# A gated mix of a recurrent-memory transformer and a GEGLU layer: one buffer for Q and K rows, P kept where P^T is written, the gate carried in the rows of b, and part of one more weight piece kept on the chip

## The chip, the cores and the metric

The kernel runs on one core of one Trainium2 chip. The metric is the device time of one launch in microseconds (us). Times of the kernel before are the median of six runs; the profile is one further execution.

## What is computed

The input x has 2048 rows of 640 numbers. Branch a cuts it into 64 segments of 32 rows. Each segment is put behind 8 memory rows, goes through attention with 32 heads of 192, and hands the first 8 rows of its result to the next segment as memory, so the segments are a strict chain. Branch b is a GEGLU layer over all rows. The output is g*a + (1-g)*b with one gate number for each row.

```python
g = sigmoid((x * gate_w).sum(-1, keepdims=True))
for s in range(64):                                # branch a
    h = concat([mem, x[:, 32*s:32*s+32]], axis=1)  # 8 + 32 = 40 rows
    q, k, v = h @ Wq, h @ Wk, h @ Wv               # 640 -> 32 heads x 192
    p = softmax(where(mask, q @ k.T * 192**-0.5, -1e9))
    o = einsum('bhte,hed->btd', p @ v, Wo)
    mem = o[:, :8];  outs.append(o[:, 8:])
b = (gelu(x @ w_gate) * (x @ w_up)) @ w_down       # branch b
return g * a + (1 - g) * b
```

## The kernel before, in words

**Order of the work.** A small scheduler (`_Sched`) takes every operation with the regions that it reads and writes, puts it on its engine's stream in program order and adds the semaphore waits. Nothing is reordered: what stands first on an engine's stream holds back what stands behind it. DMAs are issued from two streams, SP's (weights) and ACT's (`AUXQ`: scratch, b, output).

**Prologue.** Branch b comes first, in four blocks of 512 rows (`ffn_gu` and `ffn_down`, L791 to L830). `ffn_down` multiplies with `w_down` in a part of 512 columns, read out by ACT (L820), and one of 128, read out by DVE (L824); (1-g)*b goes to a scratch tensor in HBM (L828). The gate column `gcol` is spread afterwards by `gate_spread` (L731): eight small DMAs on SP build a table `gseg` with one column for each segment. Then comes the "left" phase (L880 to L908): Q and K of the last 8 rows of each segment's x, which no memory touches, for all segments at once, stored in HBM by L906. Resident weights are loaded by L656 in three classes: 35 pieces during branch b, 14 after it, 13 at the start of the first segment.

**Weights.** The four matrices are cut into 84 pieces: Wq, Wk and Wv into 4 "octs" of 5 pieces each (384 KB), Wo into 24 pieces (320 KB). They do not all fit. 62 are resident, two are "held" in PSUM and copied into SBUF buffers that are idle at that moment (L619 at q 0 and k 0, L632 at `pw`), and 20 are streamed anew for every segment through a ring of five slots (`issue_ring`, L576). A slot is loaded again when the matmuls on its old piece are done, so a piece is issued when the piece five places ahead of it has been used. A loop over estimated times (`COST`, `tcons`) picks the 20. It takes these, as (matrix, oct, piece) or (3, Wo piece): (0,0,3), (1,0,4), (0,1,1), (1,1,0), (1,1,4), (0,2,3), (1,2,1), (2,2,0), (0,3,1), (1,3,0), (2,3,0), (2,3,4), and Wo 2, 5, 8, 11, 15, 18, 21, 23.

**A segment.** The list `PROG` gives the order: q, k, v of an oct (L947, L967), with the scores (`sc`, L1009), exponent (`ex`, L1036), transposed P (`pt`, L1061), P times V (`pv`, L1087) of earlier octs between them, and Wo (L1110) at the end.

- Q and K rows: ACT copies PSUM into `rows_sb` (L951), Q into one buffer, K into another; DVE transposes each (`tq`, `tk`, L957) for the scores.
- Softmax: DVE takes the maximum and subtracts (L1024, L1026), ACT takes the exponent, DVE sums, inverts and multiplies into `p_sb` (L1043; for oct 3 L1045 and L1046). `p_transp` transposes on PE and DVE masks the result into `PTm` and `PTl` (L1064, L1067), from which `pv_oct` multiplies; ACT and DVE read its result out (L1091, L1097, L1098).
- End of a segment: DVE casts the 8 memory rows (L1155), PE transposes them (L1165), DVE writes them into H (L1170), and the next segment's q can start. Then L1176 mixes g*a into the rows of b; `out_store` sends them out, issued behind K of oct 0 of the next segment. V of oct 1 uses the same bytes as these rows, so its read-out (L978) waits for that store to land.
- GpSimd fills the left rows of Q and K from the staging buffer `stg` (L927, L929).

Every fourth segment computes V of the left rows as well (L991).

Of the kernel before, what the change touches and what calls it, by code (L numbers as in the profile page):

```python
# [221 lines left out]
def _build(nc, A_x, A_mem0, A_Wq, A_Wk, A_Wv, A_Wo, seg_len, w_gate, w_up, w_down,  # L222
# [17 lines left out]
    R = L + M  # L240
# [22 lines left out]
    b_scr = nc.dram_tensor("ffn_b_scratch", (S, Dm), BF, kind="Internal").ap()  # L263
# [4 lines left out]
    total = int(nc.sbuf_bytes_remaining) - 64  # L268
    total -= total % 64
# [8 lines left out]
    wsA["small"] = al(NSEG * 4 + 8 + 32 + 16)  # L278
    HD = Dm // 2
    wsA["ident"] = al(128 * 2)  # L280
    wsA["maskm"] = al(R * 2)
# [3 lines left out]
    wsB["rows"] = al(2 * 768)  # L285
    wsB["stg"] = al(NOCT * 2 * LW * 2)
# [5 lines left out]
    wsB["p"] = al(4 * 64 * 2)  # L292
    wsB["stats"] = al(2 * 3 * 4 * 4)
# [12 lines left out]
    ffn_sz["brow"] = al(NBR * Dm * 2)  # L306
# [4 lines left out]
    res_cap = total - wsA_total - wsB_total - ring_bytes  # L311
# [11 lines left out]
    assert o == ring_bytes + res_cap  # L323
# [24 lines left out]
    for k, n in (("gseg", 0), ("mbd", 4 * NSEG), ("mle", 4 * NSEG + 8), ("gwT", 4 * NSEG + 40)):  # L348
        wsA_off[k] = wsA_off["small"] + n
# [7 lines left out]
    gseg = fview(wsA_off["gseg"], 4 * NSEG)  # L357
    r_gseg = sreg(wsA_off["gseg"], 4 * NSEG)
# [4 lines left out]
    gwT = bview(wsA_off["gwT"], KT * 2)  # L363
    r_gwT = sreg(wsA_off["gwT"], KT * 2)
# [12 lines left out]
    rowb = bview(o_rowb, HD * 2)  # L377
    r_rowb = sreg(o_rowb, HD * 2)
# [11 lines left out]
    rows_sb = [bview(wsB_off["rows"] + b * 768, 768) for b in range(2)]  # L390
    r_rows = [sreg(wsB_off["rows"] + b * 768, 768) for b in range(2)]
    stg = bview(wsB_off["stg"], NOCT * 2 * LW * 2).rearrange("p (o m b i) -> p o m b i", m=2, b=6, i=2 * M)
    stg_flat = bview(wsB_off["stg"], NOCT * 2 * LW * 2)
    r_stg = sreg(wsB_off["stg"], NOCT * 2 * LW * 2)
# [4 lines left out]
    p_sb = bview(wsB_off["p"], 512).rearrange("p (t k) -> p t k", k=2 * L)  # L399
    pm_sb = bview(wsB_off["p"], 256).rearrange("p (t k) -> p t k", k=L)  # L400
    pl_sb = bview(wsB_off["p"] + 256, 256).rearrange("p (t k) -> p t k", k=L)
    r_p = sreg(wsB_off["p"], 512)
# [8 lines left out]
    st_f = [[fview(wsB_off["stats"] + (3 * b + i) * 16, 16) for i in range(3)] for b in range(2)]  # L411
    r_st = [sreg(wsB_off["stats"] + 48 * b, 48) for b in range(2)]
    assert NVB * 768 >= Dm * 2
    mem0r = bview(wsB_off["v"], Dm * 2)
    r_mem0r = sreg(wsB_off["v"], Dm * 2)
# [26 lines left out]
    brow = [bview(ffn_off["brow"] + b * Dm * 2, Dm * 2) for b in range(NBR)]  # L442
    r_brow = [sreg(ffn_off["brow"] + b * Dm * 2, Dm * 2) for b in range(NBR)]
# [31 lines left out]

    def piece_size(key):
        return GO if key[0] == 3 else GQ

    def piece_view(key, o):
        if key[0] == 3:  # L480
# [5 lines left out]
            ("q", 2), ("pt", 0), ("sc", 1), ("tq", 2), ("ex", 1), ("k", 2), ("tk", 2), ("pv", 0), ("v", 2),  # L486
            ("q", 3), ("pt", 1), ("sc", 2), ("tq", 3), ("ex", 2), ("k", 3), ("tk", 3), ("pv", 1), ("v", 3),
# [33 lines left out]
    HELD2 = (0, 1, 4)  # L521

# [4 lines left out]
    nstream = 0  # L527
    while True:
        streamed = set()
        for k in range(nstream):  # L530
            target = (k + 0.5) * tseg / nstream
            best = min((i for i in range(npieces) if i not in streamed and i not in held_i and may_stream(order[i])), key=lambda i: abs(tcons[i] - target))
            streamed.add(best)
        if tot_bytes - GO - GQ - sum(piece_size(order[i]) for i in streamed) <= res_cap:
            break
        nstream += 1
# [26 lines left out]
    r_ring = [sreg(o, GQ) for o in ring_off]  # L563
    order_index = {key: i for i, key in enumerate(order)}
# [6 lines left out]
    def issue_ring(seg, upto):  # L571
        done = issued.get(seg, 0)
        while done <= upto:
            key = order[stream_list[done]]
            slot = stream_counter[0] % B_RING
            S_.add("sp", lambda e, slot=slot, key=key: e.dma_start(piece_view(key, ring_off[slot]), piece_src(key)),  # L576
                   writes=[r_ring[slot]], dma_sem="ring%d" % slot, name="ring s%d p%d" % (seg, done))
            stream_counter[0] += 1
            ring_of[(seg, key)] = slot
            done += 1  # L580
        issued[seg] = done

    def piece(seg, key):
# [13 lines left out]
        slot = ring_of[(seg, key)]  # L597
        return piece_view(key, ring_off[slot]), r_ring[slot]
# [10 lines left out]
    o_held = wsB_off["rows"] + al(2 * 768) - GO  # L609
    assert o_held >= wsB_off["Q"] and o_held + 1024 >= wsB_off["rows"]  # L610
# [3 lines left out]
    assert o_held2 + GQ <= wsB_off["p"] + 256  # L614
# [44 lines left out]
    def load_residents(cls):  # L659
        for key in order:  # L660
# [70 lines left out]
    def gate_spread():  # L731
        S_.add("pool", lambda e: e.memset(gseg, 0.0), writes=[r_gseg], name="gate zero")
        for i in range(8):
            q, h = i % 4, i // 4
            S_.add("sp", lambda e, q=q, h=h: e.dma_start(gseg[64 * h + M:64 * h + R, NG * q:NG * q + NG], gcol[L * q:L * q + L, :]),
                   reads=[r_gcol], writes=[sreg(wsA_off["gseg"] + 8 * i, 8)], dma_sem="gl", name="gl%d" % i)

# [67 lines left out]
    def ffn_down(blk):  # L805
        n1 = min(Dm, 512)
        for a in range(FA):
# [3 lines left out]
            for f in range(FT):  # L811
                fns.append(lambda e, f=f, a=a, xb=xb: e.matmul(ps[:, xb, 0:n1], hT_sb[:, f, a * 128:(a + 1) * 128], wd_sb[:, f, 0:n1],  # L812
                                                               start=(f == 0), stop=(f == FT - 1)))
                if Dm > 512:
                    fns.append(lambda e, f=f, a=a, yb=yb: e.matmul(ps[:, yb, 0:Dm - 512], hT_sb[:, f, a * 128:(a + 1) * 128], wd_sb[:, f, 512:Dm],
                                                                   start=(f == 0), stop=(f == FT - 1)))
            wr = [r_ps[xb]] + ([r_ps[yb]] if Dm > 512 else [])
# [5 lines left out]
            if Dm > 512:  # L823
                S_.add("dve", lambda e, bs=bs, yb=yb, a=a: e.tensor_scalar(  # L824
                    out=brow[bs][:, 512:Dm], in0=ps[:, yb, 0:Dm - 512], scalar1=gtmp[:, 4 + a:5 + a], scalar2=None,
                    op0=ALU.mult), reads=[r_ps[yb], r_gtmp], writes=[r_brow[bs]], name="ffn b evac2")
            row0 = blk * FB + a * 128
            S_.add(AUXQ, lambda e, bs=bs, row0=row0: e.dma_start(b_scr[row0:row0 + 128, :], brow[bs]),  # L828
# [19 lines left out]
    gate_spread()  # L848
    held_buf = {HELD2: (wsB_off["Q"], wsB_off["vl"]), HELD: (wsB_off["uT"], wsB_off["stg"])}
    for a_, b_ in zip(("Q", "vl", "uT", "stg"), ("stg", "uT", "stats", "vl")):  # L850
        assert wsB_off[b_] - wsB_off[a_] >= GQ
# [70 lines left out]
    def stg_load(s):  # L922
        S_.add(AUXQ, lambda e: e.dma_start(stg_flat, qkl[s]), reads=[Rg("qk", 64 * o_ + s, 64 * o_ + s + 1) for o_ in range(NOCT)],
               writes=[r_stg], dma_sem="stg", name="stg s%d" % s)

    def left_fill(s, o):
        S_.add("pool", lambda e: e.tensor_copy(out=Qs[:, :, L:R].rearrange("p b r h -> p b (r h)"), in_=stg[:, o, 0]), reads=[r_stg], writes=[r_Ql],  # L927
               name="Ql s%d o%d" % (s, o))
        S_.add("pool", lambda e: e.tensor_copy(out=Ks[:, :, L:R].rearrange("p b r h -> p b (r h)"), in_=stg[:, o, 1]), reads=[r_stg], writes=[r_Kl],  # L929
# [99 lines left out]
    def softmax(s, o):  # L1029
# [18 lines left out]
        S_.add("dve", fns, reads=[rb, rst], writes=[r_p], name="smax p")  # L1048

    def p_transp(s, o):  # L1050
        bank = 5 + o % 2
# [20 lines left out]
    def pv_oct(s, o):  # L1072
# [17 lines left out]
        S_.add("pe", fns[8:], reads=[r_v[o % NVB], r_vl[o], r_PTm, r_PTl], writes=[r_ps[B]], name="PVb s%d o%d" % (s, o))  # L1090
        S_.add("act", lambda e: e.activation(  # L1091
# [182 lines left out]
```

## Time and profile before

| | us |
|---|---|
| six runs, median (lowest to highest) | 1890.12 (1885.56 to 1901.77) |
| the profiled execution, its own time | 1898.12 |
| its span, first to last instruction | 1896.4 |
| branch b, until the left phase starts | 0 to 175.7 |
| left phase, until the first segment's matmuls | 175.7 to 300.3 |
| first segment, until its memory rows | 300.3 to 342.4 |
| 62 segments, from memory rows to memory rows | 342.4 to 1869.4, 24.63 each |

The mean granted TensorE clock is 0.986. PE is busy for 93% of the span, DVE 49%, ACT 47%, GpSimd 8%. Busy PE is no measure of distance from the end: its ends are modelled, and it says nothing of which wait comes last. The rows to read are the waits of PE, by what ended them, and the timeline of one segment. The segments differ: the shortest takes 22.5 us, the longest 27.07; those that compute the left rows' V take 25.72 in the mean.

### The profile page before, as it was taken

Reading aid. Unit: us, or ns where it says so; the run is one execution under the profiler, and the core shown is the slowest. Engines: PE = TensorE matmul, PEld = TensorE weight load, DVE = VectorE, ACT = ScalarE, POOL = GpSimd, SP = SyncE. Lnnn points to the kernel's source line nnn. Section 1 sums busy time; section 2 is a strip of 40 time slices with the busy share of each in tenths; the row PEclk is TensorE's granted clock in tenths of the full one; section 3 lists DMA queues with packets and bytes.
Section 4 is the critical chain, followed back from the end, with each engine's and each line's share of the span. In section 5 each row is a group of like instructions: output and inputs, shape, how many; then the busy total and the mean of one; then the engine's idle time right before and its main releaser. Section 6 shows DMA issues by size and latency. Waiting matters only on the chain.

```text
span 1896.4 us, 79908 instructions
## 1 busy us (share of the span) xinstructions
PE 1755.1 (93%) x34856; PEld 1173.8 (62%) x34864; DVE 937.1 (49%) x2944; ACT 882.0 (47%) x2093; POOL 145.1 (8%) x547
## 2 busy tenths in 40 slices
PE   8999796999999999999999999999999999999998
PEld 4456684666666666666666665666666666666665
DVE  3222243555555555555555545555555555555555
ACT  2222233555444454554454444555555555554454
POOL 1000000000000000000000000000000000000000
PEclk9999898999999999999999999999999999999999
DMA  9512658999999999989999989999999999999998
GB/s 364 215 32 73 195 159 247 310 325 320 317 315 321 309 309 316 317 298 324 307 325 305 310 289 313 295 311 325 322 316 325 321 314 327 324 319 301 309 318 281
DMA packets 281737, 551.03 MB, mean 291 GB/s; under 512 B 82466, under 2 KB 107818, under 8 KB 281386
## 3 DMA queue, kind: packets, MB, share of 16 engines
q1 hardware_dynamic: 202698, 506.45, 77.9%
q10 hardware_dynamic: 78688, 39.48, 7.7%
q8 instruction: 272, 4.46, 0.9%
q14 instruction: 79, 0.65, 0.1%
HBM read 524.69 MB, written 21.10 MB: 288 GB/s over the span
## 4 chain that ended last, share of the span: by engine, by line
PE 71%; DMA 20%; DVE 4%; ACTq 2%; ACT 2%; issue 1%; SPq 0%; DVEq 0%
PE ps L947 21%; PE ps L967 12%; DMA arena<-in_A_Wo_dram 12%; PE ps L1110 11%; PE ps L890 5%; PE ps L1087 4%; PE ps L1009 3%; PE ps L794 3%; PE ps L797 3%; DMA arena<-in_A_Wv_dram 3%; DMA arena<-in_A_Wq_dram 2%; DMA arena<-in_A_Wk_dram 2%; PE ps L1001 2%; PE ps L812 2%; PE ps L991 1%; PE ps L1165 1%
## 5 line engine op out<-in xcount | busy, mean ns | idle before, releaser
L947 PE MATMUL ps<-arena 128*32 128x384 bf16 x10240 | 513.5, 333 | 25.3 <-DVE arena L1170 16.1
L1110 PE MATMUL ps<-arena 128*40 128x320 bf16 x6144 | 479.5, 300 | 38.0 <-DMA arena<-in_A_Wo_dram 33.9
L1110 PEld LDWEIGHTS ps<-arena 128*40 128x40 bf16 x6144 | 314.6, 100 | 137.8 <-DMA arena<-in_A_Wo_dram 67.2
L951 ACT ACTIVATE arena<-ps 128x384 bf16<-128x384 f32 x512 | 312.0, 609 | 140.1 <-PE ps L947 121.5
L947 PEld LDWEIGHTS ps<-arena 128*32 128x32 bf16 x10240 | 254.3, 98 | 167.9 <-DVE arena L1170 20.6
L967 PE MATMUL ps<-arena 128*32 128x384 bf16 x5800 | 293.8, 330 | 15.5 <-DMA arena<-left_xt_scratch 12.2
L957 DVE STREAM_TRANSPOSE arena<-arena 128x192 f32<-128x192 f32 x512 | 190.0, 371 | 120.9 <-ACT arena L951 120.5
L619 ACT ACTIVATE arena<-ps 128x576 bf16<-128x576 bf16 (+1 forms) x192 | 113.4, 591 | 252.2 <-PE ps L1110 238.9
L967 PEld LDWEIGHTS ps<-arena 128*32 128x32 bf16 x5800 | 147.4, 97 | 103.8 <-DMA arena<-left_xt_scratch 12.6
L978 ACT ACTIVATE arena<-ps 128x384 bf16<-128x384 f32 x256 | 125.5, 490 | 153.4 <-PE ps L967 77.1
L927 POOL COPY arena<-arena 128x96 bf16<-128x96 bf16 x256 | 68.4, 267 | 1551.1 <-PE ps L1009 819.2
L1064 DVE TENSOR_TENSOR arena<-ps,arena 128x320 bf16<-128x320 bf16 x256 | 125.5, 490 | 107.9 <-PE ps L1061 105.6
L1036 ACT ACTIVATE ps<-ps 104x160 f32<-104x160 f32 x256 | 72.8, 284 | 181.8 <-DVE ps L1026 179.2
L1087 PEld LDWEIGHTS ps<-arena 128*64 128x64 bf16 x3072 | 112.5, 125 | 57.2 <-DVE ps L1026 27.0
L1155 DVE CAST arena<-ps 104x320 bf16<-104x320 f32 x63 | 30.9, 491 | 236.4 <-PE ps L1110 236.4
L1091 ACT ACTIVATE arena<-ps 128x320 bf16<-128x320 f32 x256 | 111.8, 437 | 70.1 <-PE ps L1087 69.4
L1087 PE MATMUL ps<-arena 128*64 128x64 bf16 (+1 forms) x3072 | 136.4, 222 | 6.7 <-ACT arena L632 4.5
L1009 PE MATMUL ps<-arena 64*40 64x40 bf16 (+1 forms) x4096 | 120.4, 181 | 2.5 <-issue 1.7
L890 PE MATMUL ps<-arena 128*128 128x256 bf16 x960 | 111.0, 280 | 11.4 <-ACT arena L898 5.9
L1024 DVE TENSOR_REDUCE arena<-ps 104x4 f32<-104x160 f32 x256 | 81.0, 316 | 73.9 <-PE ps L1009 73.7
L890 PEld LDWEIGHTS ps<-arena 128*128 128x128 bf16 x960 | 95.5, 100 | 26.5 <-ACT arena L898 7.0
L1009 PEld LDWEIGHTS ps<-arena 64*40 64x40 bf16 (+1 forms) x4096 | 100.4, 97 | 11.7 <-issue 2.0
(70 smaller groups left out, 1538.8 us busy)
## 6 DMA issues: line engine op xcount, KB each, us to landing
arena<-in_A_Wo_dram SPq DMA_DIRECT2D x528, 320.0 KB, 4.5
arena<-in_A_Wk_dram SPq DMA_DIRECT2D x340, 384.0 KB, 5.0
arena<-in_A_Wq_dram SPq DMA_DIRECT2D x277, 384.0 KB, 4.8
arena<-in_A_Wv_dram SPq DMA_DIRECT2D x209, 384.0 KB, 4.9
left_qk_scratch<-arena ACTq DMA_DIRECT2D x16, 768.0 KB, 7.5
arena<-left_qk_scratch ACTq DMA_DIRECT2D x64, 192.0 KB, 5.0
arena<-in_A_x_dram SPq DMA_DIRECT2D x4, 640.0 KB, 14.2
xt_scratch<-arena ACTq DMA_DIRECT2D x4, 640.0 KB, 9.1
```

The lines of the kernel that those rows point to most:

```text
L619: S_.add("act", lambda e: e.activation(out=bview(o_held2, GQ)[:, c0:c1], in_=psb(b)[:, p0:p0 + c1 - c0], func=ACTF.Copy), reads=[r_ps[b]], ...
L890: S_.add("pe", [lambda e, k=k, g_=gs[k][0], i=i, bk=bk, hf=hf: e.matmul(ps[:, bk, 0:NL // 2].rearrange("p (g t) -> p g t", t=L), g_[:, i * ...
L947: S_.add("pe", [lambda e, j=j, k=k, gv=gv: e.matmul(ps[32 * j:32 * j + 32, bank, 0:384].rearrange("p (c i) -> p c i", i=32), Hb[hb][:, k, ...
L951: S_.add("act", lambda e: e.activation(out=rows_sb[m].rearrange("p (b i h) -> p b h i", b=6, h=2), in_=ps[:, bank, 0:384].rearrange("p (b ...
L957: S_.add("dve", lambda e: e.transpose(out=dst[:, :, 0:L], in_=rows_sb[m].bitcast(F32).rearrange("p (c r) -> p c r", r=L)), reads=[r_rows[m ...
L967: return [lambda e, j=j: e.matmul(ps[32 * j:32 * j + 32, bk, 0:384], lhs, g_[:, 384 * j:384 * (j + 1)], start=(k == 0), stop=(k == KT - 1) ...
L978: S_.add("act", lambda e: e.activation(out=v_sb[o % NVB], in_=ps[:, bank, 0:384], func=ACTF.Copy), reads=[r_ps[bank]], writes=[r_v[o % NVB ...
L1009: fns.append(lambda e, gp=gp, lo=lo, hi=hi, b=(3 * tl + c) // 2, h=(3 * tl + c) % 2, tl=tl, last=(c != 1): e.matmul(ps[gp:gp + R, bank, tl ...
L1064: S_.add("dve", lambda e: e.tensor_tensor(out=PTm, in0=apx(pv[:, 0:104], [[64, 2], [0, 4], [1, R]]), in1=apx(mbd, [[0, 2], [1, 4], [0, R]] ...
L1087: fns.append(lambda e, lhs=lhs, left=left, h=h, dst=dst, rhs=rhs: e.matmul(dst, lhs, rhs, start=not left, stop=left, tile_position=(0, 64 ...
L1091: S_.add("act", lambda e: e.activation(out=apx(u[:, 0, 0, :], [[R, 2], [3 * R, 4], [1, R]]), in_=ps[:, A, 0:2 * W].rearrange("p (c t r) -> ...
L1110: fns.append(lambda e, g_=g_, i=i, c=c, h=h, tl=tl, cc=cc, u=u: e.matmul(ps[64 * h:64 * h + R, OB, 0:HD], u[:, tl, cc, :], g_[:, i, HD * h ...
```

## The change

The SBUF layout is packed so that 1920 bytes of each partition (`GP`) come free: three quarters of Wo piece 23 are then resident, and the stream brings the last quarter of it (80 KB) instead of all (320 KB).

- `rows`: one buffer of 768 bytes for Q and K rows. The read-out of K waits for Q's transpose and the other way round.
- `p_sb` lies in the bytes of `PTm`. P of oct 1, 2 and 3 is therefore emitted later: the multiplication is put by in `p_later` and added inside `pv_oct` of the oct before, behind its matmuls. `tk` of octs 2 and 3 goes behind `pv` in `PROG`.
- Gate: a DVE copy (16 in all) puts g into two extra columns of each row of b; the scratch's rows are 1288 bytes long; `rowb` brings g along, and the mix reads it from there. `gseg` and `gate_spread`, its eight DMAs and a GpSimd memset, go. `ffn_down` splits 640 columns as 320 and 320.
- Tables are packed; `stg` moves behind `PTl`, and the held piece (0,1,4) now covers its first 256 bytes; its left fill of oct 0 has a region of its own. The buffers of the held pieces' load are laid anew.
- The streamed pieces are a written list: still 20, of which 12 of Wq, Wk and Wv (6 of Wk, where there were 5, and 2 of Wv, where there were 3) and 8 of Wo.

```diff
-    wsB["rows"] = al(2 * 768)
+    wsB["rows"] = 768
-    wsB["p"] = al(4 * 64 * 2)
-    wsB["stats"] = al(2 * 3 * 4 * 4)
...
+    GP = 3 * HD * 2
+    res_cap = total - wsA_total - wsB_total - ring_bytes - GP
...
-    rows_sb = [bview(wsB_off["rows"] + b * 768, 768) for b in range(2)]
+    rows_sb = [bview(wsB_off["rows"], 768)] * 2
-    p_sb = bview(wsB_off["p"], 512).rearrange("p (t k) -> p t k", k=2 * L)
+    p_sb = bview(wsB_off["PTm"], 512).rearrange("p (t k) -> p t k", k=2 * L)
...
+    def part_src(i):
+        src = piece_src(PART)
+        return src[:, 1, HD:Dm] if i else src.rearrange("p c n -> p (c n)")[:, 0:GP // 2]
...
-            ... ("k", 2), ("tk", 2), ("pv", 0), ("v", 2),
-            ... ("k", 3), ("tk", 3), ("pv", 1), ("v", 3),
+            ... ("k", 2), ("pv", 0), ("tk", 2), ("v", 2),
+            ... ("k", 3), ("pv", 1), ("tk", 3), ("v", 3),
...
+    PART = (3, 23)
+    STREAM = ((0, 0, 0), (0, 0, 4), (0, 2, 3), (0, 3, 0), (1, 0, 4), (1, 1, 0), (1, 1, 4), (1, 2, 1), (1, 3, 0), (1, 3, 3), (2, 2, 0), (2, 3, 3), (3, 0), (3, 2), (3, 6), (3, 8), (3, 11), (3, 17), (3, 20), (3, 23))
...
-        for i in range(8):
-            q, h = i % 4, i // 4
-            S_.add("sp", lambda e, q=q, h=h: e.dma_start(gseg[...], gcol[L * q:L * q + L, :]), ...)
...
+            S_.add("dve", lambda e, bs=bs, a=a: e.tensor_copy(
+                out=browf[bs][:, HD // 2:HD + 2:HD // 2 + 1], in_=gcol[:, ...].broadcast_to([128, 2])), ...)
...
-        S_.add("dve", fns, reads=[rb, rst], writes=[r_p], name="smax p")
+        p_later.append(lambda: S_.add("dve", fns, reads=[rb, rst], writes=[r_p], name="smax p"))
+        if o == 0:
+            p_later.pop()()
...
         S_.add("pe", fns[8:], ..., name="PVb s%d o%d" % (s, o))
+        if p_later:
+            p_later.pop()()
...
+                    w = g_[:, i, HD * h:HD * h + HD] if p != PART[1] else part_sb[:, 2 * i + h] if i + h < 2 else g_
```

## The prediction

> **What bounds the kernel now.** I first read the stretch of the 62 equal segments as one window (its columns: us, then busy time of PE, PE's weight loads, DVE, ACT and GpSimd, the granted clock, the DMA share, GB/s).
>
> ```profile
> 342.00:1870.00 1528.00, 1428.31 (x31589) 960.22 (x31583) 817.26 (x2665) 765.91 (x1861) 132.71 (x497) 0.99 0.93 315
> ```
>
> PE and the 16 DMA engines are both at 93%. Neither is full, so the segment is a PE schedule with holes in it. What ends the holes is in PE's waits (us in total, times, longest):
>
> ```profile
> PE ps L1110 <- DMA arena<-in_A_Wo_dram: 33.9, 48, 2.8
> PE ps L1165 <- DVE arena L1155: 28.3, 48, 0.6
> PE ps L947 <- DVE arena L1170: 16.1, 48, 0.4
> ...
> PE ps L890 <- ACT arena L898: 5.9, 3, 5.2
> ```
>
> The second and third rows are the turn of the memory rows, which the change leaves alone. The first is late Wo pieces; with the smaller rows for Wq, Wk and Wv and the weight loads behind them, late pieces hold PE some 44 us. To see which pieces, I set the landing of each streamed piece against the next matmul and counted the gaps that it ended. Wo 23, the last, ends one in 44 of 64 segments, 27.4 us together; Wo 18 has 8.4 us, Wo 21 5.9, Wo 15 4.8, (2,3,4) 3.5, and the other Wo pieces 1.5 or less each. With pieces of the first matrices the sum is near 65 us (a count that catches shorter gaps than the waits do). In the timeline (start, length, what) the hole stands before the last four matmuls:
>
> ```profile
> 803.26 3.21 PE L1110 MATMUL ps<-arena 128*40 128x320 bf16 x44
> 807.75 0.45 PE L1110 MATMUL ps<-arena 128*40 128x320 bf16 x4 [1.28 <-DMA arena<-in_A_Wo_dram]
> ```
>
> Why it is this piece follows from the ring: a piece is issued when the piece five places ahead has been used. I take all places from the undisturbed segment that starts at 1623.91 and lasts 22.50 us, counted from its start. Wo 8, five places ahead, is used by 17.89, and Wo 23 is needed at 22.03: a lead of 4.1 us. The issues take 4.5 us (Wo) to 5.0 us (Wk) to land:
>
> ```profile
> arena<-in_A_Wo_dram SPq DMA_DIRECT2D x528, 320.0 KB, 4.5
> arena<-in_A_Wk_dram SPq DMA_DIRECT2D x340, 384.0 KB, 5.0
> ```
>
> Leads of 4.8 (Wo 18, Wo 21) leave 6 to 8 us of holes, 4.9 (Wo 11) leaves 1.5, 5.2 ((1,0,4)) 1.0.
>
> **What the Trainium skill says.** "DMA: Bandwidth & Descriptors", section "Latency and other measured facts", gives a fixed cost of about 2 us for a DMA, growing with the load on HBM. The trace agrees in kind: 384 KB at 315 GB/s is 1.25 us, yet the landing takes 5.0, so most of it is fixed cost and the queue of the pieces ahead; removing bytes shortens the second part only. The same page, section "Issuing engines are not separate DMA queues", says that DMAs of all issuers interleave on the same 16 engines. The trace agrees: the first left store (ACT's queue) lands after 14.6 us while SP's resident loads run, and later ones after some 4.6. "Perfetto Trace Analysis", section "Identifying the Most-Contended Engine", warns that occupancy of the 16 engines misleads; so I don't read 93% as "DMA sets the time".
>
> **The change, part by part.**
>
> *Fewer bytes, other places.* The stream before is 12 x 384 + 8 x 320 = 7168 KB a segment, after it 6928: 240 KB less. At 315 GB/s that is 0.78 us of DMA time. Wo 23 now brings 80 KB, so its own transfer is 0.78 us shorter, and it is issued behind Wo 6 (used by 17.25) and not Wo 8: 0.64 us earlier. Together 1.4 us, where the mean hole is 27.4/44 = 0.62: about 24 of the 27 us go. The other places, with the same steps: Wo 20 has a lead of 5.4 and Wo 17 5.1, in the stead of Wo 21, 18 and 15: 8.4 + 5.9 + 4.8 = 19 becomes some 5. But Wo 11 now follows (2,3,3), its lead falls from 4.9 to 4.4; by the rows above (27 us at 4.1, 7 at 4.8) that is +16. (1,0,4) falls from 5.2 to 4.6: +9. Wo 6, 2 and 8 stand at 4.85, 4.9, 5.0: together 12, where Wo 2, 5 and 8 had 1.6. Sum -24 - 14 + 16 + 9 + 10 = -3. Against it stands the shorter queue: 0.78 us less work in each 24.6 shortens every landing. With about three pieces ahead of one that is issued, some 3.3% of 3 to 4 us plus the small piece's own saving for those behind it, I take 0.2 us. On the slope between 4.1 and 4.8 (29 us for each us of lead) 0.2 is 6 us for each of the two tight pieces and about 1 for each of six others: -18. Faster segments take back about 4. I take **-17 us**; ends: -3 without the shorter queue, -38 if Wo 11 and (1,0,4) cost nothing and half of the queue's gain comes (-3 - 25 - 10).
>
> *P in the bytes of P^T.* Octs 1 and 2: P comes behind `pv` and ahead of `tk`. In the undisturbed segment PV 1 ends on PE at 1637.34, and DVE reaches P (L1043) at 1637.73 behind its sum and reciprocal: no wait, nothing added. Behind P on DVE stands `tk` 3, for which the scores wait. Oct 3 has no such room:
>
> ```profile
> 1640.88 0.29 DVE L1045 TENSOR_TENSOR arena<-ps,arena 104x128 bf16<-104x128 f32 x1
> 1641.08 0.18 DVE L1046 TENSOR_TENSOR arena<-ps,arena 104x32 bf16<-104x32 f32 x1
> ...
> 1640.57 0.49 PE L1087 MATMUL ps<-arena 128*64 128x160 bf16 x12
> 1640.89 0.71 PE L1110 MATMUL ps<-arena 128*40 128x320 bf16 x8
> 1641.43 0.26 PE L1061 MATMUL ps<-arena 104*64 104x104 bf16 x4
> ```
>
> PV 2 ends at 1641.06. P now starts 0.04 later, takes 0.38, PE sees it 0.04 later: 1641.52, where PE stands ready at 1641.43. The same sum over all 62 segments gives +0.08 us in 48 and less or nothing in the rest: 48 x 0.08 = 4 us; a part hides behind late Wo pieces that follow. **+3 us** (0 to +6). The read-out of PV 2's middle (L1098, 0.31) and the mask (0.49 + 0.28) move by the same 0.1 behind it and still end at 1642.5, ahead of PV 3 at 1642.61.
>
> *One rows buffer.* K's read-out waits for Q's transpose. Oct 2, on ACT:
>
> ```profile
> 1632.55 0.49 ACT L978 ACTIVATE arena<-ps 128x384 bf16<-128x384 f32 x1 [1.82 <-PE ps L947]
> 1632.94 0.60 ACT L951 ACTIVATE arena<-ps 128x384 bf16<-128x384 f32 x1
> 1633.38 0.35 ACT L1036 ACTIVATE ps<-ps 104x160 f32<-104x160 f32 x1
> 1633.64 0.63 ACT L951 ACTIVATE arena<-ps 128x384 bf16<-128x384 f32 x1
> ```
>
> The transpose of Q 2 ends at 1633.96, so the second L951 moves from 1633.64 to 1634.00. Behind it on ACT are the read-outs of PV 0 (0.43 + 0.33), V 2 (0.50) and Q 3, which PE lets start at 1635.52; they now end at 1635.48. `tk` 2 moves by 0.08 only, for P was ahead of it on DVE; the scores have 0.3 to 0.8 us of room there. Oct 0: K's read-out moves from 1627.10 to 1627.33, and with it the issue of `out_store` behind it. The first row above, called a wait for PE, is one for that store: PE had long been done, and the store lands just before. So everything in this fence moves 0.23 later as well, 0.59 in all, on a room of 0.04 at Q 3 and 0.5 at Q 3's transpose. Octs 1 and 3 move by 0.08, inside rooms of 0.33 and 0.06 to 0.21. I take **+2 us** (0 to +25, the rival below).
>
> *Gate.* The eight DMAs take SP 5.46 us ahead of the loads for which the left phase leaves room; ACT's second left store then sits in its issue for 8.05 us while they land, and PE waits 5.2:
>
> ```profile
> 176.10 5.46 SPq L735 DMA_DIRECT2D arena<-arena  x8
> 182.78 6.87 SPq L656 DMA_DIRECT2D arena<-in_A_Wv_dram  x12
> ...
> 198.87 10.61 PE L890 MATMUL ps<-arena 128*128 128x256 bf16 x75 [5.18 <-ACT arena L898]
> ```
>
> Loads 5.5 us earlier, less 0.6 for the part piece, are done at about 198.5, not 203.4. The store is then delayed for about 8 us of overlap, not 13: **-3 us** (-5 to 0). The 16 DVE copies (L719, of the same width, takes 0.17 us) lie on DVE, which waits 50 us in `ffn_down`. Columns stay 640, PE's spacing there is 56 + 216 ns; nothing. Rows of 644 bytes move the b loads, which L1176 awaits 4.2 us in all: nothing.
>
> Sum: -17 + 3 + 2 - 3 = -15. The profiled execution would take 1898.1 - 15 = 1883; the median of the six runs is 8.0 lower, so **1875 us** (-0.8%).
>
> **Rivals.** *The DMA engines' throughput sets the pace.* For it: the 0.93, the holes at Wo. Then each segment gives back its 0.78 us, 63 x 0.78 = 49, plus 3 for the gate: 1890 - 52 = 1838; with the P and rows costs hidden and PE's floor reached in the short segments, about four fifths, 1848. Against it: landings of back-to-back pieces come about 1.0 us apart where a piece has 24.63/20 = 1.23. *The holes move.* Wo 11 and (1,0,4) wait for what Wo 23 no longer does: -3 + 3 + 2 - 3 = -1, so 1889. *Slower: the rows buffer's turn.* The 0.59 us at Q 2 passes Q 3's read-out and transpose to `tk` 3, for which the scores of oct 3 wait with a room of 0.06 to 0.21: 0.4 us x 63 = 25; PE's wait gives pieces time, so the stream's part holds at about -8, the gate's at -3: +14, 1904. It decides from 0.3 us a segment on (0.3 x 63 = 19 against 20). Against it: 0.5 us of room at Q 3's transpose in this segment; for it: stores that land later than here. That the part isn't resident is no open case: the issue rows would show it.
>
> **How the numbers follow.** Forecast 0.64, centre 1875, own range 1864 to 1886; throughput 0.14; holes move 0.11; slower 0.11. A measurement of this kernel can tell about 0.5% from no change, that is 1880.7 and 1899.6. Five sixths of the forecast lie below 1880.7: 0.53 + 0.14 = 0.67 faster; 0.11 + 0.11 = 0.22 same; 0.11 slower. The range of 1850 to 1893 leaves out most of the slow rival and half of the throughput rival.
>
> **What would show it.** The Wo row of PE's waits falls from 33.9 to some 20, and the hole moves from the last four matmuls to Wo 11. Transposes of P (L1061) of oct 3 start 0.05 us behind P in nearly all segments. Waits of the scores stay under 6 us; over 20 us would make the rows rival right. DMA share stays near 0.92; a fall of the segment to 23.9 means throughput. The 5.18 us hole before L890 shrinks to 2 or 3. I am wrong at the root if the holes at Wo keep their sum.

## The result, and the profile after

| | before | after |
|---|---|---|
| median of the runs, us | 1892.09 (64 runs) | 1886.01 (29 runs) |
| ratio, 95% interval | | 0.9964 (0.9951 to 0.9976) |
| the profiled execution, its own time | 1898.12 | 1895.56 |
| its span | 1896.4 | 1893.7 |
| one of 62 segments, mean | 24.63 | 24.55 |

The change gives 6.8 us (0.36%), where the prediction had 15. It is a gain, but it lies inside the half per cent that was called no change.

Both profiled executions are slower than the median of their kernel (by 6 and by 9.5 us), so a difference of a few us between two profiles means little by itself. The paired ratios are used for sizes, the profiles for places.

First the segments as one window, with the columns of the window shown ahead of the prediction (us, busy time of PE, its weight loads, DVE, ACT, GpSimd, clock, DMA share, GB/s):

```profile
344.90:1867.20 1522.30, 1430.33 (x31580) 958.81 (x31580) 816.53 (x2665) 773.26 (x1860) 133.02 (x496) 1.00 0.92 305
```

PE's share is 94% and the DMA share 0.92, nearly as before; the clock is 1.00 where it was 0.99. The waits of PE say more (us in total, times, longest):

```profile
PE ps L1174 <- DVE arena L1164: 28.3, 48, 0.6
PE ps L1120 <- DMA arena<-in_A_Wo_dram: 19.8, 29, 2.1
PE ps L949 <- DVE arena L1179: 15.8, 48, 0.4
PE ps L949 <- DMA arena<-in_A_Wk_dram: 7.9, 16, 1.1
...
PE ps L1094 <- ACT arena L980: 4.2, 8, 1.1
...
PE ps L969 <- ACT arena L980: 3.7, 8, 0.6
```

The Wo row fell from 33.9 to 19.8, as forecast. The Wk row was 1.2 us before and is 7.9: late pieces have moved to Wk. The two rows that name L980, the read-out of V, were not in the list before. The turn of the memory rows (first and third row) is as it was.

The transfers of the stream and of the output (KB each, median us from issue to landing):

```profile
arena<-in_A_Wo_dram SPq DMA_DIRECT2D x464, 320.0 KB, 4.5
...
arena<-in_A_Wo_dram SPq DMA_DIRECT2D x64, 80.0 KB, 4.0
...
out_dram<-arena ACTq DMA_DIRECT2D x128, 20.0 KB, 5.2
```

The 64 loads of 80 KB are the last quarters of Wo 23. A Wo piece of 320 KB still takes 4.5 us to land, so the queue has not become shorter for it. Over all streamed pieces but Wo 23 (segments 1 to 62 of each profile) the mean from issue to landing is 4.73 us; it was 4.74. The output store takes 5.2 us to land; it took 4.1 before.

The timeline of one segment shows where the Wo hole is now, and P of oct 3 (start, length, what):

```profile
829.48 0.49 PE L1094 MATMUL ps<-arena 128*64 128x160 bf16 x12
...
830.24 0.29 DVE L1047 TENSOR_TENSOR arena<-ps,arena 104x128 bf16<-104x128 f32 x1
...
830.68 0.31 PE L1120 MATMUL ps<-arena 128*40 128x320 bf16 x1 [0.17 <-DVE arena L1048]
830.68 0.28 PE L1068 MATMUL ps<-arena 104*64 104x104 bf16 x2
...
832.55 0.45 PE L1120 MATMUL ps<-arena 128*40 128x320 bf16 x4 [0.65 <-DMA arena<-in_A_Wo_dram]
832.83 0.49 PE L1094 MATMUL ps<-arena 128*64 128x160 bf16 x12
```

DVE starts P only when PV 2 (first line) is over, and PE waits 0.17 us for it ahead of the transposes (L1068). The hole of 0.65 us now stands before the four matmuls of Wo 11, just ahead of PV 3 (last line), and not before the last four of the segment. Counted by piece as for the prediction, Wo 23 fell from 27.4 us to 0.5, Wo 11 rose from 1.5 to 13.4, (1,0,4) from 1.0 to 5.8. All Wo pieces together went from 49.6 to 27.5, the pieces of Wq, Wk and Wv, without the first of the segment, which mostly coincides with the turn, from 16 to 24. (The new list has two pieces at the start, (0,0,0) and (0,0,4); only (0,0,0), 3.2 us, is left out there.)

The waits of ACT for the output store, in the kernel before and then after:

```profile
ACT arena L978 <- DMA out_dram<-arena: 33.2, 27, 2.2
```

```profile
ACT arena L980 <- DMA out_dram<-arena: 72.4, 34, 3.7
```

V of oct 1 is read out over the bytes that the store sends. Behind the memory rows the store is issued at 3.59 us in the median (3.25 before) and its second half lands at 9.18 (8.27); V's read-out starts at 9.27 (8.45). PE then waits for the PSUM bank, in PV 0 or V 2. Two things delay the store: K's read-out, which now waits for Q's transpose, and three reloads of the ring, into the slots that (0,0,0), (0,0,4) and (1,0,4) leave just ahead of it (before, only (0,0,3) and (1,0,4) left one there).

One more number goes with the gain: the granted clock, the share of full speed at which TensorE may run. It is listed for the 29 executions of the changed kernel, 0.9913 in the mean, and for 103 of the kernel before that ran beside the experiments, 0.9867. Within the kernel before, 23 executions at 0.985 or less take 1899.3 us in the mean and 17 at 0.989 or more 1886.8. At 0.989, which both kernels have, 14 executions of the kernel before take 1886.7 us and 3 of the changed one 1886.9. What lowers it in the segments are stretches of about 3.4 us at half the clock, and each follows a window of the same length in which PE stood idle for 1.2 us or more. An example from the kernel before, a hole of PE and then the windows around it (columns as above, the clock third from the end):

```profile
1158.02 0.45 PE L1110 MATMUL ps<-arena 128*40 128x320 bf16 x4 [1.24 <-DMA arena<-in_A_Wo_dram]
```

```profile
1155.83:1159.24 3.41, 1.58 (x22) 0.68 (x18) 0.49 (x1) 0.70 (x2) 0.53 (x2) 1.00 0.93 331
1159.25:1162.65 3.40, 3.11 (x41) 1.64 (x44) 1.00 (x3) 1.53 (x3) 0.00 (x0) 0.50 0.84 276
```

I divided the segments of all 16 profiles of this document into such windows, by the times of the clock's own record. Of 6947 with less than 1.2 us of PE idle none is followed by a stretch at half clock, of 63 with 1.2 to 1.5 us 8 are, of 43 with more 31. The kernel before has eight in its 62 segments, six of them behind a hole of 0.5 us or more at Wo 23, which stands just ahead of the turn of the memory rows, where PE waits again; the changed kernel has one, behind a hole of 2.1 us at Wo 11. Against segments of the same place in the cycle of four, the segments with a stretch are longer by 13 us together before and by 2 after. Those without one take 24.47 us before and 24.52 after. So by these figures the gain lies in fewer stretches at half clock, and the rest of the schedule comes out even. The runs agree: a clock lower by 0.0046 over 1890 us is 8.7 us, more than the gain of 6.8. No run here holds the clock fixed, so this is an association and not a test.

### The profile page after: what moved, and what is told of

It is laid out like the page before. It is cut to its first block, busy times and chain, and to the rows that moved or that the text cites. A ratio compares the mean times of both kernels' runs of the same rounds, so it can differ in the third digit from the quotient of the medians.

```text
span 1893.7 us, 80690 instructions
## 1 busy us (share of the span) xinstructions
PE 1758.4 (93%) x34864; PEld 1179.8 (62%) x34864; DVE 942.8 (50%) x2960; ACT 887.9 (47%) x2093; POOL 145.5 (8%) x546
## 4 chain that ended last, share of the span: by engine, by line
PE 68%; DMA 23%; DVE 4%; ACT 2%; issue 1%; ACTq 1%; SPq 0%; DVEq 0%
PE ps L949 18%; PE ps L1120 15%; PE ps L969 11%; DMA arena<-in_A_Wo_dram 10%; DMA arena<-in_A_Wk_dram 5%; PE ps L892 4%; PE ps L1094 4%; DMA out_dram<-arena 4%; PE ps L794 3%; PE ps L797 3%; DMA arena<-in_A_Wq_dram 3%; PE ps L1011 3%; PE ps L1003 2%; PE ps L993 1%; PE ps L812 1%
## 5 line engine op out<-in xcount | busy, mean ns | idle before, releaser
L1120 PE MATMUL ps<-arena 128*40 128x320 bf16 x6144 | 481.1, 300 | 23.2 <-DMA arena<-in_A_Wo_dram 19.8
L1120 PEld LDWEIGHTS ps<-arena 128*40 128x40 bf16 x6144 | 319.0, 100 | 118.4 <-DMA arena<-in_A_Wo_dram 39.0
L980 ACT ACTIVATE arena<-ps 128x384 bf16<-128x384 f32 x256 | 126.6, 495 | 183.4 <-DMA out_dram<-arena 72.4
L1094 PE MATMUL ps<-arena 128*64 128x64 bf16 (+1 forms) x3072 | 140.5, 223 | 8.4 <-ACT arena L980 4.2
L892 PE MATMUL ps<-arena 128*128 128x256 bf16 x960 | 107.7, 275 | 13.4 <-ACT arena L744 6.9
L892 PEld LDWEIGHTS ps<-arena 128*128 128x128 bf16 x960 | 93.9, 99 | 27.0 <-ACT arena L744 7.2
```

Of the source, the lines that this page charges most:

```text
L892: S_.add("pe", [lambda e, k=k, g_=gs[k][0], i=i, bk=bk, hf=hf: e.matmul(ps[:, bk, 0:NL // 2].rearrange("p (g t) -> p g t", t=L), g_[:, i * ...
L980: S_.add("act", lambda e: e.activation(out=v_sb[o % NVB], in_=ps[:, bank, 0:384], func=ACTF.Copy), reads=[r_ps[bank]], writes=[r_v[o % NVB ...
L1094: fns.append(lambda e, lhs=lhs, left=left, h=h, dst=dst, rhs=rhs: e.matmul(dst, lhs, rhs, start=not left, stop=left, tile_position=(0, 64 ...
L1120: fns.append(lambda e, w=w, c=c, h=h, tl=tl, cc=cc, u=u: e.matmul(ps[64 * h:64 * h + R, OB, 0:HD], u[:, tl, cc, :], w, start=(c == 0), sto ...
```

## The experiments

After comparing the traces I held theory A: the quarter of Wo 23 gives what was forecast or more, and the sharing of bytes (P, rows) takes it back. The rivals were that the new list takes it, that the store does, or that the quarter gives little. All ratios are to the kernel before, run on the same chip in the same rounds; 0.001 is 1.9 us. A difference of two ratios from different rounds has the intervals of both: it is good to some 5 to 9 us. Stages of a segment are means over all segments of one profile.

### One part alone on the kernel before

**quarter**: only the last quarter of Wo 23 is streamed. There is no room for the rest in that layout, so the other three quarters are read from the resident Wo 22, and the result of branch a differs. Every instruction has its old shape.

```diff
+            ... e.dma_start(*((bview(ring_off[slot], 2 * HD), piece_src(key)[:, 1, HD:Dm]) if key == PART else ...
...
+                    w = g_[:, i, HD * h:HD * h + HD] if p != PART[1] else piece_view((3, 22), res_off[(3, 22)])[:, i, HD * h:HD * h + HD] if i + h < 2 else g_
```

> The kernel before, but of Wo 23 only the last quarter is streamed (80 KB for 320 KB); the other three quarters are read from the resident Wo 22, so the result of branch a is not the reference's. List, P, rows and gate as before. Theory A (the saved bytes are worth what the prediction gave them and more): the holes before Wo 23 (27 us) go, the stage from Wo 12 to the end falls from 4.35 us (mean) to 3.8, the kernel falls by 18 to 35 us, to 1857 to 1874. Rival D (the holes move to Wo 18, 21 and 15 of the old list): the stage falls to 4.1 at most, the kernel by 3 to 12 us.

1869.39 us, ratio 0.9874 (0.9846 to 0.9901): **-24 us**. PE's waits for Wo:

```profile
PE ps L1114 <- DMA arena<-in_A_Wo_dram: 11.3, 20, 1.2
```

Wo 23's holes fall from 27.4 to 2.4 us, the other seven Wo pieces from 22 to 16, but the eleven pieces of Wq, Wk and Wv behind the first, in the places that they had, rise from 16 to 23. By this count the gain is that of Wo 23 alone, and the others come out even. The streamed pieces other than Wo 23 land after 4.74 us in the mean, as before. The executions of `quarter` have a mean clock of 0.9903; at the 2.0 us for each 0.001 that the executions of all kernels here show within a kernel, some 7 of the 24 us go with the clock. Its profile has one stretch at half clock in the segments, where the kernel before has eight.

**p_alias**: P in the bytes of P^T, computed behind PV of the oct before, `tk` behind `pv`.

```diff
-    p_sb = bview(wsB_off["p"], 512)...
+    p_sb = bview(wsB_off["PTm"], 512)...
...
-        S_.add("dve", fns, ..., name="smax p")
+        p_later.append(lambda: S_.add("dve", fns, ..., name="smax p"))
```

> The kernel before with one part of the change: P lies in the bytes of P^T, is multiplied behind PV of the oct before, and tk of octs 2 and 3 stands behind pv; the freed bytes stay unused, stream, rows and gate as before. Theory A (P of oct 3 behind PV 2 is a price on PE's path that the prediction took too small): from the start of PV 2 to Wo 8 the segment grows from 1.02 us (median) by 0.12 to 0.16, the kernel by 5 to 11 us, 1897 to 1903 beside 1892. Rival B (the growth there in the changed kernel is a follow-on of late stores and pieces): PV 2 to Wo 8 grows by under 0.05 us and the time stays within 3 us.

1896.38 us, 1.0021 (1.0002 to 1.0039): +4 us, a little under the range. The stage from PV 2 through eight matmuls of Wo and the transposes of P grew from 1.09 to 1.21 us, but the stage from Wo 12 to the end shrank from 4.35 to 3.97: the holes at Wo 15, 18, 21 and 23 fell from 46.5 us together to some 25. The stages ahead of PV 2 are some 0.16 us longer.

**rows_one**: `rows_sb = [bview(wsB_off["rows"], 768)] * 2` and its region, nothing else.

> The kernel before with one part of the change: one buffer for the rows of Q and K, nothing else. Theory A (the later read-out of K pushes the issue of the output store, and the store's landing holds V of oct 1, which holds PE at PV 0): issue of the store moves from 3.25 to about 3.5 us behind the memory rows, its landing by the same 0.3, PV 0 to the scores of oct 2 grows from 2.30 us (median) to 2.4, the kernel by 5 to 12 us. Rival C (the store lands late because the new list makes three pieces be reloaded right ahead of it, not because of the rows): issue moves by 0.3, the landing stays within 0.4 of before, the stage grows by under 0.05 us, the kernel by 0 to 4 us.

1894.2 us, 0.9989 (0.9963 to 1.0015): no cost, against theory A. The store is issued 0.33 us later, as after the whole change, and lands at 8.47 instead of 8.27; nothing on PE follows from it.

**after_early**: the changed kernel, with the store issued behind Q of oct 0 instead of K.

```diff
-                if kind == "k" and i == 0 and s > 0:
+                if kind == "q" and i == 0 and s > 0:
                     out_store(s - 1)
```

> The changed kernel with the output store of the segment before issued behind the read-out of Q of oct 0 and not behind that of K. Theory A (the store's landing is what V of oct 1, Q of oct 2 and PV 0 wait for): the issue moves from 3.6 to about 2.5 us behind the memory rows, V of oct 1 is read out about 0.8 to 1 us earlier, PV 0 to the scores of oct 2 falls from 2.65 us (median) to 2.3, the kernel by 10 to 20 us, to 1866 to 1876. Rival E (late pieces take the place of that wait, or the mix's wait for the rows of b now holds ACT): the stage falls, but the kernel by under 4 us.

1883.11 us, 0.9944 (0.9925 to 0.9963). ACT's wait for the store is back where it was (31.6 us in all). The stage from PV 0 to the scores of oct 2 goes from 2.84 to 2.58 us (2.57 before the change). That is 16 us of stage time for about 4 us of run time, and the interval overlaps that of the whole change: rival E's mark is the one that is met. That pieces which land meanwhile make up for most of such a stall is likely, but not shown.

### The list against the sharing

The quarter alone gives 24 us, the whole change 7. Four kernels ask where 17 us go.

**quarter_newlist**: `quarter` with the `STREAM` tuple of the change. It moves as many bytes as `quarter` (535.70 and 535.30 MB).

> The kernel before with the last quarter of Wo 23 alone streamed (its other three quarters read from resident Wo 22, so branch a differs) and the new list of streamed pieces; rows, P, gate and tables as before. A: as with the old list, 1867 to 1872. B: 1878 to 1884, with holes at Wo 11 of 10 us or more.

1884.43 us, 0.9947 (0.9923 to 0.9971): **14 us lost by the list alone** (give or take 7). Wo 11 has 12 us of holes, (0,0,0) and (0,0,4) have 6.9 together, (1,3,3) 5.5, and the store takes 5.1 us to land, with K's rows still in a buffer of their own. With the old list (`quarter`) it takes 4.5. So the later landing is the list's doing, not the rows buffer's.

**quarter_p_rows**: `quarter`, `p_alias` and `rows_one` together, old list.

> The kernel before with its old list, the quarter of Wo 23 (three quarters read from resident Wo 22), P in the bytes of P^T and one rows buffer; gate, tables and prologue as before. Alone, P gave +4 and rows -2 us while late Wo 23 stood behind them. A: without that cover both show, +12 to +15 over the quarter alone: 1880 to 1884. B: they stay as small as alone, 1869 to 1874. Stage from PV 2 to its eighth next Wo matmul: 1.2 us in both, against 1.05 of the quarter alone.

1880.99 us, 0.9918 (0.9888 to 0.9947): 8 us over the quarter alone, half of what A asked and more than B did.

**after_oldlist**: the changed kernel with the 20 pieces that the kernel before had picked.

```diff
-    STREAM = ((0, 0, 0), (0, 0, 4), (0, 2, 3), (0, 3, 0), (1, 0, 4), ...
+    STREAM = ((0, 0, 3), (0, 1, 1), (0, 2, 3), (0, 3, 1), (1, 0, 4), (1, 1, 0), (1, 1, 4), (1, 2, 1), (1, 3, 0), (2, 2, 0), (2, 3, 0), (2, 3, 4), (3, 2), (3, 5), (3, 8), (3, 11), (3, 15), (3, 18), (3, 21), (3, 23))
```

> The changed kernel with the list of streamed pieces of the kernel before (Wo 23 still by its last quarter). The quarter alone gave -24 us on the kernel before, the whole change -6, so some 17 us are lost on the way. Theory A (the sharing costs it: P behind PV 2, some 9 us at its stage once no late Wo 23 hides it, the store behind K 5 us, the prologue 2.5): the old list changes nothing, 1883 to 1887. Rival B (the new list costs it: Wo 11 ends holes of 13 us, and three reloads ahead of the store): 1872 to 1878.

1878.54 us, 0.9909 (0.9883 to 0.9935), 17 us under the kernel before and 10 us better than the change with its own list. Rival B's mark is met within a us, and theory A alone falls.

**after_oldlist_early**: the same with the early store.

> The changed kernel with the list of the kernel before and the output store issued behind Q of oct 0 and not behind K. A: 2 to 4 us under the changed kernel with the old list and the store where it was, so 1879 to 1884. B: 1868 to 1875. If the store matters only because the new list reloads three pieces ahead of it, it gives nothing here: the same as with the store behind K, within 2 us.

1879.95 us, 0.9913 (0.9886 to 0.9941): nothing. If the store matters, it is only with the new list's reloads ahead of it.

### Which part of the list

**after_wo_old** takes the new list's twelve pieces of Wq, Wk and Wv with the old list's eight of Wo, **after_qkv_old** the reverse.

> The changed kernel with the new list's pieces of Wq, Wk and Wv and the old list's pieces of Wo. Of the new list's price of some 8 to 14 us, theory L (lead): Wo 11 costs it, because the piece five places ahead of it, (2,3,3), is used late; here it is (1,3,3) and the lead is longer: holes at Wo 11 under 3 us, 1878 to 1882. Rival S (store): the three reloads of oct 0 that come ahead of the output store cost it, and they stay: 1884 to 1888.

1902.42 us, 1.0076 (1.0052 to 1.0099): slower than the kernel before, and outside both expectations. PE's waits for pieces:

```profile
PE ps L949 <- DMA arena<-in_A_Wk_dram: 14.9, 23, 1.9
PE ps L949 <- DMA arena<-in_A_Wq_dram: 10.1, 19, 1.3
...
PE ps L1120 <- DMA arena<-in_A_Wo_dram: 3.6, 10, 0.8
```

Wo 11 is cured (1.0 us), as theory L said, but the ring is a circle: what is late on Wo now sets the start of the next segment. (0,0,4) follows Wo 15, (1,0,4) follows Wo 18; by the undisturbed segment of the kernel before their leads are 22.50 + 2.04 - 20.12 = 4.4 us each ((1,0,4): 22.50 + 2.85 - 20.94). They have 13.5 and 16.4 us of holes. (The clock of this kernel, 0.9882, is also below that of the change; at 2.0 us for 0.001 that is some 6 us.) I had looked at the lead of one piece and not gone round.

> The changed kernel with the old list's pieces of Wq, Wk and Wv and the new list's pieces of Wo. L: Wo 11 now follows (2,3,4), which is used later than (2,3,3): its holes grow to 13 us or more, 1885 to 1890. S: the store has one reload less ahead of it and lands at some 8.6 us as with the old list: 1877 to 1881.

1885.98 us, 0.9973 (0.9955 to 0.9991): as the whole change. The store lands early again (second half at 8.08 us), and that brings nothing, since Wo 11 now follows (2,3,4) with a lead of 4.2 us and has 17.3 us of holes, Wo 2 7.5:

```profile
PE ps L1120 <- DMA arena<-in_A_Wo_dram: 21.5, 35, 1.6
```

So theory L holds for the pieces that it named, S as the whole cause does not. Leads and holes over the kernels with the quarter: 4.2 us, 17.3; 4.4 us, 13.4 (the change), 13.5 and 16.4; 4.7 us, 5.8; 4.8 us, 5.4 and 4.2 (Wo 18 and 21 with the old list); 4.9 us, 2.3. One piece falls out of this row: Wo 8 in `after_qkv_old` has a lead of 4.1 us and only some 4 us of holes. It lands after 3.9 us there in the median, where Wo 11 takes 4.4. A lead has to be set against the landing at its own place. How the list's 10 to 14 us divide between late pieces and the late store stays open: both mend only together with the whole old list.

**after_oldlist_pt**: `after_oldlist` with the transposes of P of oct 3 one step later and PV 3 behind two pieces of oct 2.

```diff
-            ... ("pw", 1), ("wo", 1, 0), ("pt", 3),
-            ("wo", 1, 1), ("wo", 1, 2), ("pv", 3), ("wo", 2), ("wo", 3)]
+            ... ("pw", 1), ("wo", 1, 0), ("wo", 1, 1), ("pt", 3),
+            ("wo", 1, 2), ("wo", 2, 0), ("pv", 3), ("wo", 2, 1), ("wo", 2, 2), ("wo", 3)]
```

> The changed kernel with the whole old list and another order at the end of a segment: the transposed P of oct 3 behind Wo 8 and 9 and not ahead of them, and PV 3 behind Wo 12 and 13. P behind PV 2 then has four matmuls more of cover on PE, and the mask as many as before. If P in the bytes of P^T costs the 0.15 to 0.18 us that its stage shows (some 8 to 10 us in all), they come back: 1869 to 1873. If late pieces behind it hide most of it: 1876 to 1879. If the read-out of PV 3 comes too late for Wo 18, which it now has four matmuls less to cover: over 1881.

1869.86 us, ratio 0.9914 (0.9892 to 0.9935). The median of the runs falls in the first range; but the kernel before was quicker in those rounds too, and the ratio is that of `after_oldlist`. From PV 2 to the end a segment takes 6.30 us in the profile and not 6.45, 9 us over 62; the runs don't show it. Inconclusive.

### P or the rows buffer

**quarter_p** and **quarter_rows** put each sharing alone on `quarter`, where no late Wo 23 hides it.

> The kernel before with the quarter of Wo 23 (three quarters read from resident Wo 22) and P in the bytes of P^T, nothing else. The quarter alone gave -24, with P and the rows buffer -15.5. If P is what costs (theory P): the stage behind PV 2 is 0.15 us or more longer and the time is -14 to -18, ratio 0.9905 to 0.9926. If the rows buffer costs (theory R): -21 to -25, ratio 0.9868 to 0.9889.

1873.67 us, 0.9906 (0.9871 to 0.9940).

> The kernel before with the quarter of Wo 23 (three quarters read from resident Wo 22) and one rows buffer, nothing else. Theory P: as the quarter alone, -21 to -25. Theory R: -14 to -18, with the store some 0.3 us later and longer waits of PE for the read-outs of K or V.

1864.99 us, 0.9875 (0.9838 to 0.9911). Theory P, by the marks: P costs 0.0032 of 1892, **6 us**, and the rows buffer nothing. The intervals of these two overlap, so the runs alone don't settle it; the stage shows where P's cost lies: from PV 2 through eight matmuls of Wo it is 1.05 us in `quarter`, 1.04 in `quarter_rows`, 1.22 in `quarter_p` and in `quarter_p_rows`.

**after_half_p**: the changed kernel with the old list, half of Wo 23 resident, and P in 512 bytes of its own, multiplied where the kernel before does it.

```diff
-    GP = 3 * HD * 2
+    GP = 2 * HD * 2
...
+    o_p = o_part - 512
...
-    p_sb = bview(wsB_off["PTm"], 512)...
+    p_sb = bview(o_p, 512)...
```

> The changed kernel with the old list, half of Wo 23 resident (the stream brings 160 KB of it) and P in 512 bytes of its own, in the order of the kernel before; one rows buffer, gate and tables as changed. With three quarters resident and P shared the ratio was 0.9909. Theory P: P's 8 us come back, and of the quarter's gain some 5 go, since a landing 0.5 us earlier covers less of the hole of 0.62: 0.988 to 0.990. Theory R: 0.992 to 0.994. Holes at Wo 23: between 3 and 9 us.

1872.15 us, 0.9899 (0.9861 to 0.9937). It lands inside theory P's range, the stage behind PV 2 is 1.08 us, Wo 23 has 4.1 us of holes. The interval is too wide to put it ahead of `after_oldlist`. With `after_oldlist`, `after_oldlist_early` and `after_oldlist_pt` it is one of four whole versions that beat the kernel before by 16 to 19 us, and the change by 9 to 12. Their clocks (0.990 to 0.992) are close to that of the change, so this gain over it is not the clock's.

## Why the prediction was half right

The direction held, by the figures above through fewer stretches at half clock, of which the prediction knows nothing. The pieces that the sum named moved as it said. The size failed: one term of the sum was not there, and others were mis-sized.

*Wo 23, -24.* Right in the count: `quarter` gives -24, its holes go from 27.4 to 2.4 us, and to 0.5 with the earlier issue of the new list. The agreement is partly luck, for some 7 of the 24 us of run time go with the clock, which the prediction doesn't have.

*The other places, -14 + 16 + 9 + 10 = +21.* Right in direction, too high in size. Against sums of 17.5 us at Wo 11, 10 at (1,0,4), 12 at Wo 6, 2 and 8 and 5 at Wo 20 and 17, the holes came out at 13.4, 5.8, 6.8 and 6.5: +9 and not +21. The slope of 29 us for each us of lead was drawn through places whose pieces land differently, after 4.7 us (Wo 23, Wo 18) and 3.8 (Wo 11) in the profile before. ((1,0,4) has a lead of 4.7 by the segment that was used, not 4.6.) The whole of the list costs 10 (`after` against `after_oldlist`) to 14 us (`quarter_newlist` against `quarter`), with pieces that the sum did not name.

*The shorter queue, -18, and the faster pace, +4.* **This is the step that failed.** I took 0.2 us off every landing, and nothing came off: the mean of the streamed pieces other than Wo 23 is 4.74 us before, 4.74 in `quarter` and 4.73 after the change. In `quarter`, with all places unchanged, the other Wo pieces lost 6 us of holes and the pieces of Wq, Wk and Wv gained 7: net +1. (Of the -18, 12 stood at Wo 11 and (1,0,4) in their new places, which `quarter` does not have, so +1 is to be set against some -6 + 4.) A likely reason is that a shorter segment asks for its bytes sooner: 0.78 us of transfer went, the segment of `quarter` became 24.09 instead of 24.63 us, and the DMA share stayed at 0.93. No run tests that reason.

Here the prediction also left a gap: it costed one of the new list's pieces of Wq, Wk and Wv, and took the store's landing from the kernel before. (0,0,0) and (0,0,4) lie ahead of the store, which lands 1.1 us later after its issue. So the stream as a whole (-24 and the list), forecast at -17, came to -10 to -14: the +21 that was too high made up for much of the -14 that was not there.

*P in the bytes of P^T, +3 (0 to +6).* Right in its place, under in size. The prediction had PE start the transposes 0.46 us behind the end of PV 2; the median is 0.49 and the mean 0.56, against 0.38 and 0.44 before. That is 0.12 us in nearly all segments, not 0.08 in 48: 7 us. Runs: +4 on the kernel before, +6 on `quarter`; the intervals don't tell these apart.

*One rows buffer, +2 (0 to +25).* Right: -2 and 0 in the two kernels that have it alone. The rival that made it decide the sign named the scores of oct 3; they did not wait.

*Gate, -3 (-5 to 0).* Right at the hole that it named: PE's hole before L892 is 3.1 us instead of 5.2. But the next one, which the prediction left out, grew from 5.3 to 6.9:

```profile
198.98 8.44 PE L892 MATMUL ps<-arena 128*128 128x256 bf16 x75 [3.08 <-ACT arena L900]
```

```profile
PE ps L890 <- ACT arena L744: 5.3, 1, 5.3
```

```profile
PE ps L892 <- ACT arena L744: 6.9, 1, 6.9
```

The two together take 9.5 us in the mean of the eight profiles with the new gate and 10.3 in the eight with the old one. The left phase takes 122.6 us against 124.7, -2, with 9.4 us of it at half clock against 13.2. In the pair shown the first memory rows come 2.5 us later after the change: branch b ends 2.2 us later, which it does or doesn't in profiles of both kinds, the left phase is 3.6 us shorter, and the first segment 3.7 us longer, with 23.9 us of it at half clock and not 13.7.

*The sum.* Predicted -24 + 21 - 14 + 3 + 2 - 3 = -15. Measured by the experiments: -24 (Wo 23 with whatever its queue and its clock gave) + 14 (list) + 6 (P) + 0 (rows) - 2 (gate, by profiles) = -6, against -6.8. The four that come from runs are good to 5 to 9 us each, so agreement within 1 us is luck.

*The rivals.* Throughput as the pace is refuted: `quarter` and `quarter_newlist` move the same bytes and lie 14 us apart, and so do `after_oldlist` and `after_wo_old` (535.6 and 536.0 MB), 32 us apart. "The holes move", which I gave 1889, is nearest in time, and right about Wo 11 and (1,0,4), though the holes did not keep their sum. The clock stands in no rival.

## What to carry to other kernels

In a ring, a late piece is a matter of the lead between its issue and its use: work out the lead for every piece, set it against the landing at that place, and go all round the ring into the next iteration, before moving one. Taking bytes out of the stream helped the piece that was late here and left the landing of the others at 4.7 us, so don't book a shorter queue for them without a trace that shows one. Look at the granted clock beside the holes: here a hole that brought PE's idle time to more than 1.5 us in 3.4 was followed by a stretch at half clock in 31 of 43 cases. And cost a new wait without the stall behind which it hides, if the same change removes that stall.

## What the runs showed that I had not expected

The landing of a 20 KB store on ACT's queue goes with the weight loads that SP issues just ahead of it: 4.1 us in the kernel before, 4.5 with the quarter and the old list, 5.1 and 5.2 with the new list (4.8 with the store issued earlier), 5.2 with the new list's pieces of Wq, Wk and Wv alone and 4.0 with its Wo pieces alone. That DMAs of both issuers share the engines was cited in the prediction for the left stores, and I had not drawn the conclusion for this one.

Stalls don't add: 16 us of stage time behind PV 0 were worth about 4 us of run time (`after_early`, 8 at most by the intervals).

A hole can cost more than its length: the eight stretches at half clock in the kernel before, behind holes at Wo 23 and 21 and the turn, go with segments that are 13 us longer in all, 1.6 for each stretch of 3.4 us.
